# Gated linear attention feeding a gated FFN: decays of five units fetched through DRAM, a planner that counts tiling changes, and a new plan

## The chip, the cores and the metric

The kernel runs on one core of one Trainium2 chip. The metric is the device time of one execution in microseconds (us); the lower, the better.

## The reference

Two stages run one after the other. The first is a linear attention with a decay per key channel, the second a feed-forward network (FFN) whose gate is a relu. With B = 4 batches, H = 8 heads, S = 768 tokens and D = 48 channels:

```python
f = 1.0 / (1.0 + np.exp(-f_logit))
for t in range(S):
    state = f[:, :, t, :, None] * state + np.einsum('bhd,bhe->bhde', k[:, :, t], v[:, :, t])
    y[:, :, t] = np.einsum('bhd,bhde->bhe', q[:, :, t], state)
x = y.transpose(0, 2, 1, 3).reshape(B * S, H * D)      # 3072 x 384
gate = np.maximum(x @ w_gate, 0.0)                     # 384 -> 1536
val = x @ w_val
out = gate * val @ w_out                               # 1536 -> 384
```

Inputs and output are float32.

## The kernel before

**Work.** The tokens of one batch are cut into chunks of 128. Two neighbouring chunks of a batch make a unit, so there are 12 units, taken in the order `seq`: units 0 to 3 are the first pair of chunks of batches 0 to 3, units 4 to 7 the second pair, units 8 to 11 the last. Within a unit, a partition holds two neighbouring tokens, which is why most things exist twice (i = 0, 1 for the token in the partition, y = 0, 1 for the chunk).

A unit runs through these steps:
- four loads of 384 KB (f, k, q, v), queued on SP;
- exp and ln of the gate on ScalarE (L620, L622), then sums over the tokens of a chunk on TensorE ("cum", L629 and L630);
- exponentials of the sums, one for q and one for k, per i (L641, L644, L651), and the products with q and k, called hats (L663 or L669);
- the hats are turned by TensorE with an identity (L703) and copied out of PSUM as qkT, for the units in the set `pe_hats`; for the other units a DMA turns them (L725);
- scores on TensorE (L739), masked into ptm (L747 to L752);
- "total" (L759 and L763): nine small matmuls that sum the gate over a chunk; ScalarE takes the exponential of that sum as the decay `dec` (L768);
- "state" (L777, or L787 for units of `pe_hats`) sums k times v; VectorE adds the old state (`ssum`, L594) and GpSimd multiplies by the decay (`st`, L597);
- "intra" (L819, or L826 and L830) makes the attention output, which goes to xT either by a copy (the chunks in `pe_x`) or by a copy and a DMA transpose (L848).

Two units make a group of four chunks, 512 tokens. For every group the FFN runs over 12 slices j of the hidden width: three matmuls for the gate and three for val (L866), relu on ScalarE (L872), the product gT on VectorE (L878); then the output matmuls (L894), a copy into osb and a store. In group 0 the slices j = 0 to 4 are run separately for unit 0 (256 columns) and unit 1, the slices 5 to 11 for both at once.

**Order.** The instructions of every engine are in an order that `Plan.schedule` works out when the kernel is built: it plays the program forward with written-in costs (`occ`, `lat`, and `Rings` for the DMA) and always takes the operation that can start first, at a tie the one with the lower `prio`. `pace` ties the first "cum" of a unit to an FFN slice, `first` gives the order of the first loads; `wg2@f2` puts a weight behind the landing of f of unit 2. Weights are loaded and cast by DMAs that GpSimd issues. Each engine then waits on semaphores where an operand comes from elsewhere. Until a planned 24 us, matmuls on zeros ("fillers", L958) are put into planned gaps of TensorE.

TensorE works on three tilings: whole (128 rows), rows (L739 on 48 rows, L787 on 64) and columns (L819, 32 columns).

Of the kernel before, what the change touches and what calls it, by code (L numbers as in the profile page):

```python
# [13 lines left out]
class Op:  # L14
# [4 lines left out]
                 "after", "follows", "flow", "goal", "floor", "ring", "descs", "deps0", "crosses", "slack", "tiles", "port", "early", "held")  # L19

    def __init__(self, eng, emit, reads, writes, occ, lat, prio, opens=(), after=(), follows=()):
        self.eng, self.emit, self.reads, self.writes = eng, emit, reads, writes
        self.occ, self.lat, self.prio, self.opens = occ, lat, prio, list(opens)
        self.after, self.follows = list(after), list(follows)
        self.users = []
        self.inc = False
        self.sem = None
        self.val = 0
        self.start = None
        self.flow = None  # L30
        self.ring = "hw"
        self.descs = 0
        self.floor = 0.0
        self.crosses = False
        self.slack = 0.0
        self.port = False
        self.held = False
        self.early = 0
# [13 lines left out]
class Rings:  # L52
# [27 lines left out]
    def worked(self, t):  # L80
        work = t - self.now
        for p in self.PAUSES[self.passed:]:
# [5 lines left out]
    def later(self, work):  # L88
        t = self.now
        for p in self.PAUSES[self.passed:]:  # L90
# [6 lines left out]
    def next(self):  # L97
        found = None
        for r, q in self.queue.items():
            if q:  # L100
                t = self.later(self.left[r] / self.speed(r))
# [6 lines left out]
    def step(self, t, ring):  # L108
        speeds = {r: self.speed(r) for r in self.RATE}
        for r, q in self.queue.items():  # L110
            if q:
                self.left[r] -= self.worked(t) * speeds[r]
# [17 lines left out]
class Plan:  # L130
# [3 lines left out]
    EASY = 26.0  # L134
    hot_until = 0.0
# [43 lines left out]

    def schedule(self, banks):  # L180
# [9 lines left out]
        free = dict(self.free0)  # L190
        waiting = {e: [] for e in self.ENGINES}
# [34 lines left out]
        while True:  # L226
            pick = None
            for e in self.ENGINES:
                for op in waiting[e]:
# [13 lines left out]
                    key = (at, op.prio, op.idx)  # L243
# [14 lines left out]
            (at, _, _), op, slot = pick  # L258
            e = op.eng
            waiting[e].remove(op)  # L260
# [92 lines left out]
def bass_hgrn2_outer__then__ffn_reglu_kernel(  # L353
# [23 lines left out]
    wsteps = 4  # L377
    WJ = NJ // wsteps
# [25 lines left out]
    vrest = [sb(f"vrest{i}", [128, HD], BF16) for i in range(NV // 2)]  # L404
    st = [[sb(f"st{b}_{i}", [128, SW], BF16) for i in range(2)] for b in range(B)]
# [12 lines left out]
    gT = [sb(f"gT{i}", [128, NJ, GT], BF16) for i in range(NG)]  # L418
    NR = 4
# [14 lines left out]
    pl = Plan({'bc': 3, 'tp': 2, 's': 4, 'y': 1, 'kv': 2, 'f': 4})  # L434
    pl.EASY = 34
# [61 lines left out]
    for name, t, cols, value, prio in (("halves", halves, 4, 1.0, -27), ("other", other, 64, 1.0, -26), ("away", away, 16, 16.0, -26)):  # L497
# [8 lines left out]
        ["ident"], ["ident"], occ=0.25, prio=-28)  # L506
    fill("DVE", "zeros", zeros[:], 0.0, 256, -30)
# [29 lines left out]
    def load(n, u, after=()):  # L537
# [4 lines left out]
        behind = list(after) + (sent[-5:][:1] if len(sent) >= 5 else [])  # L542
        op = chain("load", "SP", lambda: sy.dma_start(dst, src), [], [f"{n}{u % NL}"], occ=0.65, lat=1.3, prio=u * 20 - 40, after=behind)
        dma(op, f"{n}{u % NL}", 1.27, 1, 1024)
# [5 lines left out]
    def load_w(nm, s, after):  # L550
        if nm == "wo":
            src = bass.AP(tensor=w_out.tensor, offset=s * WJ * 128 * DM,
                          ap=[[DM, 128], [128 * DM, WJ], [1, DM]])
            dst = wo[:, s * WJ:(s + 1) * WJ, :]
        else:
            src = bass.AP(tensor=wsrc[nm].tensor, offset=s * WJ * 128,
                          ap=[[DFF, 128], [128 * DFF, NK], [1, WJ * 128]])
            dst = (wg if nm == "wg" else wv)[:, :, s * WJ * 128:(s + 1) * WJ * 128]
        op = chain("load_w", "POOL", lambda: gp.dma_start(dst, src), [], [f"{nm}{s}"], occ=0.79, lat=2.3,
                   prio=-10 if s == 0 else 30, after=after)  # L560
        dma(op, f"{nm}{s}", 6.0 / wsteps, ring="sw")
        return op

    done = {}

    def begin(items):
        for item in items:
            item, _, behind = item.partition("@")
            need = [done[x] for x in behind.split("&")] if behind else []
# [3 lines left out]
    t4 = lambda t: t[:, 0:HD].rearrange("p (n j e) -> p n j e", n=NP, j=2)  # L573
    QROW = NQ * 4 * NP * C

# [6 lines left out]
    def new_state(kv, u, y, P):  # L582
# [4 lines left out]
        dk = [f"dec{ai}"]  # L587
# [15 lines left out]
    def unit(u):  # L603
# [11 lines left out]
        on.update({0: {'kps': True, 'qps': True, 'q0': 'POOL', 'q1': 'POOL', 'even': 'PE', 'm00': 'DVE', 'm01': 'POOL', 'm10': 'DVE', 'tk': 'DVE', 'm11': 'DVE', 'r1': 'ACT', 'tq': 'ACT', 'v11': 'DVE', 'v10': 'DVE1', 'r0': 'POOL', 'v01': 'POOL', 'v00': 'DVE', 'x1': 'ACT', 'o1': 'DVE', 'o0': 'DVE', 'x0': 'DVE'}, 1: {'kps': True, 'r0': 'ACT', 'm01': 'DVE', 'm00': 'DVE', 'tq': 'ACT', 'v11': 'DVE', 'even': 'PE', 'tk': 'DVE', 'q1': 'POOL', 'v00': 'ACT', 'm11': 'DVE', 'r1': 'DVE1', 'm10': 'POOL', 'v01': 'ACT', 'v10': 'POOL', 'q0': 'POOL', 'qps': True, 'x1': 'ACT', 'o0': 'DVE', 'o1': 'DVE', 'x0': 'DVE'}, 2: {'tk': 'ACT', 'v01': 'POOL', 'kps': True, 'r1': 'DVE1', 'r0': 'ACT', 'even': 'DVE', 'q0': 'POOL', 'v00': 'ACT', 'v10': 'ACT', 'm00': 'DVE', 'v11': 'DVE1', 'm01': 'DVE', 'm11': 'DVE', 'tq': 'ACT', 'q1': 'POOL', 'm10': 'POOL', 'qps': False, 'o1': 'DVE', 'x1': 'DVE', 'o0': 'DVE', 'x0': 'DVE'}, 4: {'v10': 'ACT', 'v01': 'ACT', 'm00': 'DVE', 'q11': 'DVE', 'q00': 'POOL', 'q01': 'POOL', 'q0': 'POOL', 'kps': True, 'even': 'DVE', 'm01': 'DVE', 'v00': 'DVE1', 'm10': 'POOL', 'q10': 'POOL', 'q1': 'POOL', 'm11': 'POOL', 'v11': 'POOL', 'qps': True, 'tq': 'DVE', 'r0': 'POOL', 'tk': 'DVE', 'r1': 'POOL', 'o1': 'DVE', 'o0': 'DVE', 'x0': 'DVE'}, 10: {'m00': 'POOL', 'm10': 'DVE', 'q0': 'DVE', 'kps': True, 'q10': 'DVE', 'm01': 'POOL', 'q11': 'DVE', 'q00': 'POOL', 'v11': 'ACT', 'even': 'DVE', 'v01': 'DVE1', 'v00': 'POOL', 'q01': 'POOL', 'q1': 'POOL', 'm11': 'DVE', 'v10': 'DVE1', 'qps': True, 'o1': 'ACT', 'o0': 'DVE'}, 9: {'v11': 'DVE1', 'v10': 'POOL', 'even': 'DVE', 'kps': True, 'q1': 'POOL', 'm10': 'DVE', 'v00': 'DVE1', 'm11': 'POOL', 'q11': 'POOL', 'm00': 'DVE', 'q00': 'POOL', 'q10': 'POOL', 'q0': 'POOL', 'q01': 'POOL', 'v01': 'ACT', 'o1': 'ACT', 'x1': 'ACT'}, 3: {'kps': True, 'm00': 'POOL', 'm11': 'POOL', 'v11': 'ACT', 'm10': 'POOL', 'tk': 'DVE', 'v01': 'POOL', 'r1': 'ACT', 'tq': 'ACT', 'q1': 'DVE', 'v00': 'DVE1', 'v10': 'ACT', 'q0': 'DVE', 'r0': 'POOL', 'm01': 'POOL', 'even': 'PE', 'qps': True, 'x0': 'DVE', 'o1': 'DVE', 'x1': 'ACT', 'o0': 'DVE'}, 5: {'q1': 'POOL', 'm00': 'POOL', 'kps': True, 'q11': 'POOL', 'v10': 'ACT', 'v00': 'ACT', 'even': 'PE', 'q01': 'POOL', 'm11': 'DVE', 'q00': 'POOL', 'q0': 'POOL', 'v11': 'DVE1', 'm01': 'DVE', 'q10': 'POOL', 'v01': 'ACT', 'm10': 'DVE', 'tq': 'DVE', 'r0': 'DVE1', 'tk': 'ACT', 'r1': 'POOL', 'qps': False, 'x0': 'ACT', 'o1': 'ACT', 'x1': 'ACT', 'o0': 'ACT'}, 11: {'q0': 'POOL', 'v01': 'ACT', 'q10': 'POOL', 'm00': 'POOL', 'q01': 'POOL', 'm11': 'POOL', 'q1': 'POOL', 'q00': 'POOL', 'kps': True, 'v11': 'POOL', 'm01': 'DVE', 'q11': 'POOL', 'even': 'DVE', 'v00': 'POOL', 'm10': 'DVE', 'v10': 'POOL', 'x1': 'ACT', 'o1': 'ACT', 'o0': 'ACT'}, 7: {'v10': 'POOL', 'kps': True, 'q1': 'POOL', 'v01': 'ACT', 'q11': 'POOL', 'm00': 'DVE', 'v11': 'DVE1', 'even': 'DVE', 'm10': 'POOL', 'm11': 'DVE', 'm01': 'DVE', 'q10': 'POOL', 'qps': False, 'q01': 'POOL', 'o1': 'DVE', 'x1': 'DVE', 'q00': 'POOL'}, 8: {'m10': 'DVE', 'v11': 'ACT', 'q01': 'POOL', 'm01': 'POOL', 'even': 'DVE', 'q0': 'POOL', 'v10': 'ACT', 'q1': 'POOL', 'm00': 'DVE', 'kps': True, 'q11': 'POOL', 'q00': 'POOL', 'qps': False, 'o0': 'DVE'}, 6: {'v10': 'DVE1', 'v01': 'DVE1', 'q10': 'DVE', 'm10': 'POOL', 'kps': True, 'q1': 'POOL', 'even': 'PE', 'q01': 'DVE', 'm00': 'POOL', 'm01': 'POOL', 'q11': 'DVE', 'q00': 'POOL', 'm11': 'DVE', 'qps': True, 'o0': 'DVE', 'o1': 'DVE'}}.get(u, {}))  # L615
# [63 lines left out]
        v4 = by_i["v"]  # L679
        for y in range(2):  # L680
            vi = vis[y]
            for i in range(2):
# [49 lines left out]
        for y in range(2):  # L732
# [9 lines left out]
            chain("scores", "PE", scores, both, sj, occ=0.26, lat=PE_L, prio=P + 5, opens=sj)  # L742
# [12 lines left out]
        tot = Bank("kv")  # L755
        ny = 1 if last else 2

        def total():
# [292 lines left out]
```

## Time and profile before

| | us |
|---|---|
| median of 3 runs (lowest, highest) | 196.26 (196.06, 196.44) |
| profiled execution, its own time | 196.28 |
| its span, first to last instruction | 194.5 |
| TensorE busy | 187.0 (96%) |
| VectorE busy | 131.1 (67%) |
| ScalarE busy | 123.2 (63%) |
| GpSimd busy | 75.2 (39%) |

The page of the profile lists, in this order: busy time by engine, the span in 40 slices, the DMA queues, the chain of work that ended last, the costliest groups of instructions, and the DMA issues. In a timeline each row has the start, the length, the engine, the source line, the operation, "out<-in" with shapes, and how many instructions were merged into the row; in brackets stands how long the engine had been idle before and what released it. SPq stands for SP's queue issuing a DMA. A row's length at TensorE includes the pipeline, so the distance between the starts of two rows is the time that the first one took from the engine.

### The profile page before, as it was taken

The numbers are of one execution on the slowest core, as the hardware profiler recorded it, in microseconds if no ns is written. First come the engines' busy times: TensorE is split into PE (matmuls) and PEld (weight loads), VectorE is DVE, ScalarE is ACT, GpSimd is POOL, SyncE is SP. The second block draws the span as 40 slices with busy tenths as digits, with TensorE's granted clock in tenths as the row PEclk, the third lists the DMA queues.
The fourth block names the chain that finished last, engine by engine and source line by source line (L and its number), as shares of the span: only waits on it lengthen the run. The fifth ranks groups of instructions, "written<-read, shape, count | busy, mean of one in ns | idle before, by whom it ended". The sixth has DMA issues, their size and how long they took to land.

```text
span 194.5 us, 4615 instructions
## 1 busy us (share of the span) xinstructions
PE 187.0 (96%) x1827; PEld 104.7 (54%) x1850; DVE 131.1 (67%) x247; ACT 123.2 (63%) x239; POOL 75.2 (39%) x105
## 2 busy tenths in 40 slices
PE   7988999999999999999999999999999999999995
PEld 2355684655655545555555555555455455544564
DVE  4589975875799896996699976337988533442310
ACT  4997769888398999959597455336364633344312
POOL 5286458058518624096468852000056210000000
PEclk9999999999999999999999999999999999999999
DMA  6999999995999899899965472201344301111113
GB/s 163 325 290 201 255 264 193 213 275 154 318 282 286 214 323 304 185 226 219 305 186 116 80 148 66 66 16 40 93 96 89 82 18 28 44 40 40 40 43 119
DMA packets 74469, 31.36 MB, mean 161 GB/s; under 512 B 66640, under 2 KB 74448, under 8 KB 74448
## 3 DMA queue, kind: packets, MB, share of 16 engines
q1 hardware_dynamic: 69648, 27.53, 55.5%
q0 software_dynamic: 4800, 3.54, 12.0%
q8 instruction: 14, 0.23, 0.5%
q14 instruction: 7, 0.06, 0.1%
HBM read 25.95 MB, written 4.72 MB: 158 GB/s over the span
## 4 chain that ended last, share of the span: by engine, by line
PE 73%; ACT 11%; DVE 10%; issue 3%; DMA 2%; POOL 0%; SPq 0%; DVEq 0%
PE ps L866 37%; PE ps L894 21%; PE ps L819 3%; PE ps L958 3%; DVE ptm L752 2%; PE ps L703 2%; ACT relu L872 2%; PE ps L739 2%; DVE hats L669 2%; DVE gT L878 2%; DMA qkT<-hats 2%; ACT ptm L747 1%; ACT expo L644 1%; ACT f_in L620 1%; ACT ps L651 1%
## 5 line engine op out<-in xcount | busy, mean ns | idle before, releaser
L878 DVE TENSOR_TENSOR gT<-relu,ps 128x512 bf16<-128x512 bf16 (+1 forms) x77 | 49.4, 649 | 33.4 <-PE ps L866 30.2
L872 ACT ACTIVATE relu<-ps 128x512 bf16<-128x512 f32 (+1 forms) x77 | 43.7, 570 | 31.5 <-PE ps L866 31.0
L866 PE MATMUL ps<-xT,wv 128*128 128x512 bf16 (+1 forms) x225 | 58.0, 365 | 0.8 <-issue 0.5
L866 PE MATMUL ps<-xT,wg 128*128 128x512 bf16 (+1 forms) x216 | 56.2, 364 | 1.1 <-DVE st L589 0.2
L894 PE MATMUL ps<-wo,gT 128*128 128x384 bf16 (+2 forms) x300 | 52.0, 320 | 0.0
L894 PEld LDWEIGHTS ps<-wo,gT 128*128 128x128 bf16 x300 | 27.8, 98 | 18.6
L866 PEld LDWEIGHTS ps<-xT,wv 128*128 128x128 bf16 x231 | 21.4, 98 | 22.3 <-DVE ptm L752 0.4
L866 PEld LDWEIGHTS ps<-xT,wg 128*128 128x128 bf16 x231 | 21.4, 98 | 19.3 <-DVE st L589 0.4
L749 POOL TENSOR_TENSOR ptm<-ptm,seen 128x512 bf16<-128x512 bf16 x20 | 22.8, 1154 | 23.1 <-ACT ptm L747 23.1
L597 POOL TENSOR_TENSOR st<-ssum,dec 128x384 bf16<-128x384 f32 x16 | 13.3, 830 | 42.7 <-DVE ssum L594 39.5
L752 DVE TENSOR_TENSOR ptm<-ps,seen 128x512 bf16<-128x512 f32 x28 | 17.8, 683 | 2.4 <-PE ps L739 2.3
L474 ACT ACTIVATE osb<-ps 128x384 f32<-128x384 f32 (+2 forms) x10 | 4.6, 459 | 16.5 <-PE ps L894 16.5
L475 DVE COPY osb<-ps 128x384 f32<-128x384 f32 x15 | 8.3, 554 | 8.3 <-PE ps L894 8.2
L669 DVE TENSOR_TENSOR hats<-k_in,ps 64x384 bf16<-64x384 f32 x24 | 13.2, 550 | 0.6 <-ACT ps L651 0.3
L747 ACT ACTIVATE ptm<-ps 128x512 bf16<-128x512 f32 x20 | 11.1, 598 | 4.1 <-PE ps L739 4.0
L669 POOL TENSOR_TENSOR hats<-q_in,expo 64x384 bf16<-64x384 f32 x12 | 11.9, 995 | 1.3 <-ACT expo L644 0.6
L651 ACT ACTIVATE ps<-ps 128x384 f32<-128x384 f32 x24 | 10.8, 484 | 0.0
L620 ACT ACTIVATE f_in<-f_in 128x768 f32<-128x768 f32 x12 | 10.1, 840 | 1.1 <-DMA f_in<-in_f_logit_dram 1.0
L474 ACT ACTIVATE xT<-ps 128x384 bf16<-128x384 f32 x11 | 6.6, 601 | 6.2 <-PE ps L819 5.9
L958 PE MATMUL ps<-zeros 128*128 128x512 bf16 x31 | 9.7, 461 | 0.6 <-DVE hats L663 0.6
L622 ACT ACTIVATE bneg<-f_in 128x768 bf16<-128x768 f32 x12 | 10.1, 841 | 0.1
L474 ACT ACTIVATE vpad<-v_in 64x384 bf16<-64x384 f32 x19 | 9.9, 520 | 0.3
(83 smaller groups left out, 200.8 us busy)
## 6 DMA issues: line engine op xcount, KB each, us to landing
f_in<-in_f_logit_dram SPq DMA_DIRECT2D x12, 384.0 KB, 5.0
v_in<-in_v_dram SPq DMA_DIRECT2D x12, 384.0 KB, 5.0
k_in<-in_k_dram SPq DMA_DIRECT2D x12, 384.0 KB, 5.0
q_in<-in_q_dram SPq DMA_DIRECT2D x12, 384.0 KB, 5.1
out_dram<-osb SPq DMA_DIRECT2D x15, 192.0 KB, 2.6
out_dram<-osb SPq DMA_DIRECT2D x16, 96.0 KB, 2.2
wg<-in_moe_w_gate_dram POOLq DMA_DIRECT2D x4, 288.0 KB, 5.7
wv<-in_moe_w_val_dram POOLq DMA_DIRECT2D x4, 288.0 KB, 6.8
```

Source lines behind the costliest of these rows:

```text
L474: return sc.activation(out, src, AF.Copy)
L597: add(e, lambda: engine[e].tensor_tensor(t4(s_new), t4(tmp), rate, ALU.mult), [key] + dk, [f"S{b}_{y}"], prio=P + 2, **(dict(occ=0.79, lat ...
L651: add("ACT", lambda i=i, ex=ex: sc.activation(bc[i].ap[:, 0:HD] if in_place else ex[:, 1, :], bc[i].ap[:, 0:HD], AF.Exp, scale=1.0), [bc[i ...
L669: op = add(e, lambda i=i, n=n, x=x, e=e, y=y, lo=lo, exps=exps: engine[e].tensor_tensor(hats[64 * i:64 * i + 64, hi, y, x, :, 0:D], by_i[n ...
L747: add("ACT", lambda pt=pt, s=sj[j]: sc.activation(pt, s.ap[:, :].rearrange("p (n t) -> p n t", n=NP), AF.Copy), [sj[j]], [f"raw{mis[y]}_{j ...
L749: add("POOL", lambda pt=pt, mask=mask: gp.tensor_tensor(pt, pt, mask, ALU.mult), [f"raw{mis[y]}_{j}", "seen"], [f"raw{mis[y]}_{j}", f"ptm{ ...
L752: add("DVE", lambda pt=pt, mask=mask, s=sj[j]: ve.tensor_tensor(pt, s.ap[:, :].rearrange("p (n t) -> p n t", n=NP), mask, ALU.mult), [sj[j ...
L866: mm = te.matmul(bank.ap[:, 0:n], wt[:, kt, j * 128:(j + 1) * 128], xT[xi][:, kt, n0:n1], start=(kt == 0), stop=(kt == NK - 1))
L872: add("ACT", lambda: sc.activation(relu[ri][:, 0:n], gate.ap[:, 0:n], AF.Relu), [gate], [f"relu{ri}"], prio=P, **act_t(n))
L878: add("DVE", lambda: ve.tensor_tensor(gT[gi][:, j, n0:n1], relu[ri][:, 0:n], val.ap[:, 0:n], ALU.mult), [val, f"relu{ri}"], [f"gT{gi}_{j}_ ...
L894: mm = te.matmul(bank.ap[:, 0:cut[1] - cut[0]], gT[gi][:, j, r * C:(r + 1) * C], wo[:, j, cut[0]:cut[1]], start=(j == 0), stop=(j == NJ - 1))
L958: return te.matmul(bank.ap[:, 0:WARM], zeros[:, 0:128], zeros[:, 0:WARM], start=True, stop=True, skip_group_check=True)
```

## The change

**Decays through DRAM.** For units 7 to 11 (the entry `td` of a unit's table) the nine matmuls of "total" and their exponential are gone. Partitions 63 and 127 of the q exponential (i = 1) hold the decay of the two chunks. SP writes these rows to a DRAM tensor `rates` and, when that has landed, reads them back as columns of 4-byte elements into `dec`, with two transfers for each chunk. Unit 7 has five such transfers; units 8 to 11 need one chunk only and have three.

**The planner.** Each TensorE operation has a mode (whole, rows or columns). At a tie in the start time the planner takes an operation of the present mode first, and a change of mode costs 0.095 us in the plan. The costs of several operations, the limits of PSUM banks by kind, the slack on a DMA's landing (1 to 1.5 us) and the pauses of the DMA queues are changed too.

**Units.** `pe_hats` loses unit 4: its hats are turned by DMAs, and its "state" is done on 128 rows. `pe_x` and `q_lined` name other units.

**Start.** The loads go in another order, up to eight in flight instead of five; the first weight is put behind k of unit 1, the ninth load, where it was behind f of unit 2, the sixth. In group 0 only the slices j = 0 to 2 are run for each unit alone.

**Plan.** `pace`, the table that says which engine does a copy, mask or product, and a few priorities are new. An added path that spreads v by matmuls (`vpe`) and one that loads weights uncast (`raw_w`) are switched on for no unit and no weight.

```diff
+    TURN = 0.095
+    STAYS = False
+    def stay(self, mode, new):
+        if mode == "whole" or new == "whole":
+            return 2
+        return 0 if new == mode else 1 if self.STAYS else 2
...
-                    key = (at, op.prio, op.idx)
+                    key = (at, self.stay(mode, op.mode) if e == "PE" else 2, op.prio, op.idx)
...
+            if e == "PE":
+                if op.mode != mode:
+                    at = max(free[e] + self.TURN, at)
+                mode = op.mode
...
-    first = 'f0 v0 f1 k0 q0 f2 wg2@f2 wg0@f2 wv0@f0 wv1@v0 k1 wg1@k1 q1 wv2@q1 v1 k2@wv0 q2 wg3@q2 wv3@v0 wo1@f0 wo0@f1 wo2@f0 wo3@f0 f3@wg2 q3@wv0 k3@wg1 v2@wo1 v3@wv0'.split()
+    first = 'f0 k0 v0 q0 v1 f1 q3 q1 k1 wg0@k1 wv0@k0 wg1@f0 wv1@k0 wg2@f0 wv2@q0 wg3@q3 wo0@k0 wv3@f0 q2 wo2@q2 wo3@k0 wo1@f1 f2 k2 f3 k3@wg0 v2 v3'.split()
-    pe_hats = {0, 1, 2, 3, 4, 5}
-    pe_x = {0, 1, 2, 3, 4, 5, 6, 7, 9, 10, 11, 12, 13, 21, 22, 23}
-    q_lined = {0, 1, 4, 7, 8, 9, 10}
+    pe_hats = {0, 1, 2, 3, 5}
+    pe_x = {0, 1, 2, 3, 4, 5, 7, 8, 9, 10, 11, 12, 13, 15, 22, 23}
+    q_lined = {0, 1, 3, 5, 7, 8, 9, 10}
...
-    pl = Plan({'bc': 3, 'tp': 2, 's': 4, 'y': 1, 'kv': 2, 'f': 4})
-    pl.EASY = 34
+    pl = Plan({'bc': 3, 'tp': 1, 's': 4, 'y': 3, 'kv': 4, 'f': 4, 'hot': 1, 'vp': 1})
+    pl.EASY = 30
...
-        behind = list(after) + (sent[-5:][:1] if len(sent) >= 5 else [])
+        behind = list(after) + (sent[-8:][:1] if len(sent) >= 8 else [])
...
+        if on.get("td") and not qb and 2 * u >= NA:
+            at = 2 * u * HD
+            op = add("SP", lambda at=at: sy.dma_start(
+                bass.AP(tensor=rates, offset=at, ap=[[HD, ny], [1, HD]]),
+                bass.AP(tensor=expo, offset=63 * EROW + (ei * 2 + 1) * 2 * HD, ap=[[64 * EROW, ny], [1, HD]])),
+                [f"expq{ei}_1"], [f"rates{u}"], occ=0.36, lat=0.9, prio=P + 2.4)
+            dma(op, f"rates{u % 4}", 0.15, 1, 2)
+            for y in range(ny):
+                for j in range(2):
+                    row = bass.AP(tensor=rates, offset=at + y * HD + j * D, ap=[[1, D], [2 * D, NP]])
+                    col = bass.AP(tensor=dec_all, offset=64 * j * DROW + (a0 + y) * NP * 2 + j, ap=[[DROW, D], [2, NP]])
+                    op = add("SP", lambda row=row, col=col: sy.dma_start(col, row, allow_slow_non_contiguous=True), [f"rates{u}"],
+                             [f"dec{a0 + y}" + "_1" * j], occ=0.5, lat=0.9, prio=P + 2.5)
+                    dma(op, f"dec{a0 + y}_{j}", 0.8, 1, 192)
+        else:
+            tot = Bank("kv")
...
-                op.slack = 1 if op.flow is not None else 0
-        for r0, r1, js in {0: [(0, 2, range(0, 5)), (2, 4, range(0, 5)), (0, 4, range(5, 12))]}.get(g, [(0, GC, range(NJ))]):
+                op.slack = 1.5 if op.flow is not None else 0
+        for r0, r1, js in {0: [(0, 2, range(0, 3)), (2, 4, range(0, 3)), (0, 4, range(3, 12))]}.get(g, [(0, GC, range(NJ))]):
...
-    pace = {4: 0, 6: 22, 9: 29, 8: 32, 10: 46, 5: 6, 7: 18, 11: 44}
+    pace = {6: 21, 10: 24, 5: 3, 8: 31, 9: 23, 11: 49}
```

More of the change, by code (lines that the diff above doesn't have):

```diff
@@ L36, in __init__ @@
         self.port = False
+        self.mode = "whole"
         self.held = False
@@ L86, in worked, with later @@
         return work
-    def later(self, work):
+    def later(self, work, ring):
         t = self.now
+        if ring == "sw":
+            return t + work
         for p in self.PAUSES[self.passed:]:
@@ L741, in scores @@
                 return mm
-            chain("scores", "PE", scores, both, sj, occ=0.26, lat=PE_L, prio=P + 5, opens=sj)
+            held = [f"{n}{(2 * u - 1) % NM}_{j}" for j in range(2) for n in ("raw", "ptm")] if on.get("pr") and u else []
+            chain("scores", "PE", scores, both + held, sj, occ=0.225, lat=PE_L, prio=P + 5, opens=sj).mode = "rows"
             for j in range(2):
```

150 lines of the change are left out of this document (104 added, 46 removed).

## The prediction

> **What bounds the kernel now.** I read the page first (its busy times and the chain that ended last), then the waits of TensorE, then the timeline of TensorE from start to end.
>
> ```profile
> span 194.5 us, 4615 instructions
> PE 187.0 (96%) x1827; PEld 104.7 (54%) x1850; DVE 131.1 (67%) x247; ACT 123.2 (63%) x239; POOL 75.2 (39%) x105
> ...
> PEclk9999999999999999999999999999999999999999
> ...
> PE 73%; ACT 11%; DVE 10%; issue 3%; DMA 2%; POOL 0%; SPq 0%; DVEq 0%
> ...
> L958 PE MATMUL ps<-zeros 128*128 128x512 bf16 x31 | 9.7, 461 | 0.6 <-DVE hats L663 0.6
> ```
>
> TensorE is the bound: busy 96% of 194.5 us, at the full granted clock in every slice, and 73% of the chain. Of the 187.0 us, 9.7 are fillers on zeros, all in the start. A busy engine can still be one that waits inside its pipeline, so the waits come next.
>
> ```profile
> PE ps L950 <- DVE zeros L462: 1.3, 1, 1.3
> PE ps L787 <- ACT qkT L474: 0.6, 1, 0.6
> ```
>
> The longest wait, 1.3 us, is the very first instruction; those with useful work behind them are 0.6 us and less (the list goes on with shorter ones). So once the FFN has begun there is next to nothing to win from waits. The time can only fall if TensorE gets less to do, loses less between its instructions, or begins earlier.
>
> ```profile
> 1.65 4.47 PE L958 MATMUL ps<-zeros 128*128 128x512 bf16 x10
> ...
> 20.38 0.50 PE L866 MATMUL ps<-xT,wg 128*128 128x256 bf16 x3 [0.22 <-DVE st L589]
> 20.98 0.50 PE L866 MATMUL ps<-xT,wv 128*128 128x256 bf16 x3
> 21.31 0.49 PE L866 MATMUL ps<-xT,wg 128*128 128x256 bf16 x3
> ...
> 184.18 7.99 PE L894 MATMUL ps<-wo,gT 128*128 128x384 bf16 x60
> ```
>
> The useful stretch reaches from 20.38, the first FFN matmul, to 184.18 + 7.99 = 192.17. After it only the last copy and store remain, 194.5 - 192.17 = 2.33 us, which the change leaves as they are. The profiled execution took 196.28 us, 1.78 more than its span and 0.02 from the median of 196.26; I keep both constant and sum against 196.28.
>
> **The change, part by part.**
>
> *Nine matmuls fewer, five times.* The cost of one "total" is the distance between starts:
>
> ```profile
> 33.41 0.17 PE L759 MATMUL ps<-away,other 128*128 128x16 bf16 x1
> 33.43 0.34 PE L763 MATMUL ps<-halves,bneg 128*128 128x4 bf16 x8
> 33.63 0.81 PE L866 MATMUL ps<-xT,wg 128*128 128x512 bf16 x3
> ```
>
> 33.63 - 33.41 = 0.22 us. Units 7 to 11 run after 20.38, where TensorE has no idle time, so the whole of it counts: 5 x 0.22 = **-1.10 us**.
>
> *Unit 4 leaves TensorE's transposes.* Its 16 transposes and its "state" in row tiling stand together:
>
> ```profile
> 55.95 1.06 PE L703 MATMUL ps<-ident,hats 128*128 128x128 bf16 x16
> ...
> 57.39 0.82 PE L866 MATMUL ps<-xT,wv 128*128 128x512 bf16 x3
> ...
> 81.09 0.50 PE L777 MATMUL ps<-vpad,hats 128*128 128x96 bf16 x8
> 81.43 0.81 PE L866 MATMUL ps<-xT,wv 128*128 128x512 bf16 x3
> ```
>
> 57.39 - 55.95 = 1.44 us go, with the two changes of tiling inside; the "state" of a unit on 128 rows, 81.43 - 81.09 = 0.34 us, comes instead: **-1.10 us**. In exchange SP issues two more DMA transposes. Those of the other units show what that can cost TensorE at worst so far:
>
> ```profile
> qkT<-hats SPq DMA_TRANSPOSE x12, 3.2
> ...
> 116.94 0.62 PE L739 MATMUL ps<-qkT 48*128 48x128 bf16 x16 [0.42 <-DMA qkT<-hats]
> ```
>
> Landing takes 3.2 us, and one of twelve was late, by 0.42 us. I put 0 to 0.42 for unit 4; the cover is FFN work of the group before, and without it the 3.2 us would be seen whole.
>
> *Changes of tiling.* Here TensorE goes from FFN to scores and back:
>
> ```profile
> 68.48 0.81 PE L866 MATMUL ps<-xT,wg 128*128 128x512 bf16 x3
> 69.23 0.62 PE L739 MATMUL ps<-qkT 48*128 48x128 bf16 x16
> 69.78 0.82 PE L866 MATMUL ps<-xT,wv 128*128 128x512 bf16 x3
> ...
> 21.73 0.41 PE L819 MATMUL ps<-ptm,vpad 128*32 128x128 bf16 x16
> 22.23 0.50 PE L866 MATMUL ps<-xT,wv 128*128 128x256 bf16 x3
> ...
> 22.99 0.35 PE L819 MATMUL ps<-qkT,st 128*32 128x128 bf16 x12
> ...
> 23.50 0.50 PE L866 MATMUL ps<-xT,wv 128*128 128x256 bf16 x3
> ...
> 157.76 0.66 PE L894 MATMUL ps<-wo,gT 128*128 128x384 bf16 x3
> ```
>
> Three wide FFN matmuls take 0.65 us in a steady run, so the scores could have begun at 69.13; they begin at 69.23. One change costs about 0.10 us. Between the start of the FFN and the end I count 54 changes in the timeline, the first at 21.73 and the last at 157.76; two of them went with unit 4 above. How many of the other 52 the new order saves cannot be read from the trace. At least the intra pairs of units 4 and 11 are now tied together (the entry `yy`), which is 4 changes, 0.4 us; if the rule joins score, state and intra work of neighbours it could be 20, 2.0 us. I take 10: **-1.0 us**. [...]
>
> *The FFN's narrow slices.* 24 matmuls on 256 columns become 12 on 512: eight runs of three at 0.33 us (20.98 to 21.31 is such a step) against four of 0.65 us. Nothing.
>
> *The start.* Weights now wait for the ninth load instead of the sixth.
>
> ```profile
> 9.07 1.11 SPq L543 DMA_DIRECT2D v_in<-in_v_dram  x1
> ...
> 10.63 1.70 POOL L559 DMA_DIRECT2D wg<-in_moe_w_gate_dram  x2 [3.86 <-DMA f_in<-in_f_logit_dram]
> ...
> v_in<-in_v_dram SPq DMA_DIRECT2D x12, 384.0 KB, 5.0
> ...
> wg<-in_moe_w_gate_dram POOLq DMA_DIRECT2D x4, 288.0 KB, 5.7
> wv<-in_moe_w_val_dram POOLq DMA_DIRECT2D x4, 288.0 KB, 6.8
> ```
>
> The ninth load was issued at 9.07 and takes 5.0 us, so the first weight is asked for at about 14.07 instead of 10.63, 3.44 us later. wg0 then lands at 14.07 + 5.7 = 19.8, wv0, issued 0.85 later, at 21.7. FFN began at 20.38, so the gates can still begin in time: four of them (the PSUM limit of the FFN) fill 4 x 0.33 = 1.3 us and val follows at 21.7. If the gates run first this costs nothing; if they alternate with val as before, up to 21.7 - 20.38 = 1.3 us. Against it: unit 0 gets k as the second load and q as the fourth, and unit 1 has its four loads by 14 us, so both intra runs of unit 1, from 21.73 to 22.23 and from 22.99 to 23.50, 1.0 us together, can move ahead of the FFN into time that fillers hold now. Bounds -1.0 to +1.3; I take **+0.2**, the middle.
>
> *The DRAM trip.* A decay now takes a write, a wait on SP, a read. Nearest row: a 96 KB store.
>
> ```profile
> out_dram<-osb SPq DMA_DIRECT2D x16, 96.0 KB, 2.2
> ...
> 100.41 0.88 ACT L644 ACTIVATE expo<-ps 128x384 f32<-128x384 f32 x2
> ...
> 106.94 0.82 POOL L597 TENSOR_TENSOR st<-ssum,dec 128x384 bf16<-128x384 f32 x1
> ...
> 142.62 0.87 ACT L644 ACTIVATE expo<-ps 128x384 f32<-128x384 f32 x2 [1.53 <-DVE ps L633]
> ...
> 150.07 0.83 POOL L597 TENSOR_TENSOR st<-ssum,dec 128x384 bf16<-128x384 f32 x1 [1.61 <-DVE ssum L594]
> ```
>
> Two trips are 4.4 us. For unit 8 the q exponentials end at 101.29 and the decay is used at 106.94: 5.6 us of cover; for unit 11 from 143.49 to 150.07, 6.6 us. So it is hidden if SP is free to issue, by a margin of about 1 to 2 us. These are 5 + 4 x 3 = 17 more DMAs on SP's queue, and the reads are behind a wait: output stores, the DMA transposes of the same units and late loads queue behind it. I take +0.3 for new stalls of this kind and of unit 4, with 0 and 2.2 (one landing seen whole) as ends.
>
> Sum: 196.28 - 1.10 - 1.10 - 1.0 + 0.2 + 0.3 = **193.6 us**.
>
> **The rivals.**
>
> *The weights are late (slower).* Place: before the first FFN matmul. If the FFN start follows the gate in full, TensorE runs fillers 3.44 us longer. The tiling gains may then also be small (0.4): 196.28 - 2.20 - 0.4 + 3.44 + 0.3 = **197.4**. It decides from a delay of about 2.6 us on, where it eats the sure savings. For it: the first weight does leave 3.4 us later. Against it: the gate weight's landing at 19.8 is still ahead of 20.38.
>
> *SP's queue (slower).* SP waits at its head for `rates` to land, 2.2 us for each of five units, with qkT transposes behind it. TensorE's order is fixed, so it stops at the scores, as it did for 0.42 us at 116.94. If the five waits are seen whole, 11 us less what covers them; if two are, 193.6 + 4.4 - 0.3 = **197.7**. [...] Against it: only a few SP instructions stand behind, and each landing has 1.5 us of slack in the plan.
>
> *VectorE takes over (no change).*
>
> ```profile
> 100.00:110.00 10.00, 9.95 (x76) 5.41 (x77) 9.72 (x18) 6.81 (x17) 8.96 (x11) 1.00 0.45 96
> ```
>
> VectorE (third pair of numbers) is busy 9.72 of 10 us while units 8 and 9 are prepared. If that stretch sets the pace, what TensorE saves for units 7 to 9 and by tilings comes back as waits. Left are unit 4's 1.10 and two totals, 0.44; with the start at its late end that is 196.28 - 1.10 - 0.44 + 1.3 = **196.0**. Against it: TensorE is busy 9.95 there.
>
> *The planner's rule does nothing.* It acts on exact ties only. Then the tiling term is 0: 194.6, inside the forecast's own range.
>
> **How the numbers follow.** The forecast with its tiling and start bounds (191.5 to 195.5) gets 0.65, late weights 0.13, SP's queue 0.09, VectorE 0.13, of which 0.06 falls below the 0.4 us, 0.05 within and 0.02 above. A difference of 0.2% (0.4 us) is about what can be told from no change here. Faster: 0.65 + 0.06 = 0.71; same 0.05; slower 0.13 + 0.09 + 0.02 = 0.24. The range goes from 191.5 to 197.4, which leaves out most of the SP case and the far ends of the others.
>
> **What would show it.** Right: no L759 and L763 for units 7 to 11, 80 transposes by L703, below 45 changes of tiling after the first FFN matmul, that matmul at 20 to 21.7 us, TensorE's waits still below 1 us each, the st of L597 released by ssum. Wrong: an FFN start at 23 us or later with more fillers than 9.7 us; the scores or st waiting for a DMA; a gap of TensorE after 100 us released by VectorE; a number of tiling changes near 52.

## The result, and the profile after

| | before | after |
|---|---|---|
| median (lowest, highest), us | 196.19 (196.06, 196.44) | 194.54 (193.87, 195.06) |
| profiled execution, its own time, us | 196.28 | 193.87 |
| span, us | 194.5 | 192.1 |
| tiling changes of TensorE, whole span / behind the first val | 62 / 53 | 51 / 39 |
| first gate, first val, end of TensorE, us | 20.38, 20.98, 192.17 | 21.65, 23.32, 189.74 |

The ratio of after to before is 0.991 (0.989 to 0.993): faster by 1.65 us, four runs each. The forecast was 193.6 within 191.5 to 197.4. All times in this document are those of fast executions; one slow execution, 200.79 us of the kernel with earlier first weights, is left out.

The page of after:

```profile
span 192.1 us, 4498 instructions
PE 183.4 (95%) x1755; PEld 101.6 (53%) x1777; DVE 129.2 (67%) x238; ACT 121.6 (63%) x233; POOL 82.5 (43%) x110
...
PEclk9999999999999999999999999999999999999999
...
GB/s 154 325 325 274 214 205 205 204 230 248 235 311 285 207 320 232 309 239 160 172 258 230 172 154 118 84 77 61 62 5 149 41 44 0 41 43 41 43 42 123
...
PE 71%; DMA 12%; DVE 8%; POOL 4%; issue 2%; ACT 1%; SPq 1%; DVEq 0%
...
L646 POOL TENSOR_TENSOR st<-ssum,dec 128x384 bf16<-128x384 f32 x16 | 13.2, 828 | 24.7 <-DMA dec<-rates 12.0
```

TensorE is still the bound, at a mean granted clock of 1.000. How much work it lost can't be read from the busy times (187.0 and 183.4): the trace of before lacks the records of 21 FFN matmuls, that of after 20. A second profile of the same kernel, the first experiment below, lacks none (it has as many matmuls as weight loads):

```profile
PE 185.5 (97%) x1777; PEld 101.8 (53%) x1777; DVE 129.2 (67%) x238; ACT 121.6 (63%) x233; POOL 82.4 (43%) x110
```

In the chain, DMA has gone from 2% to 12%. GpSimd now waits 12.0 us for the decays. Whether that matters is read from TensorE's waits (total, count, longest):

```profile
PE ps L1042 <- DVE zeros L492: 1.3, 1, 1.3
PE ps L770 <- DVE hats L712: 1.0, 2, 0.6
PE ps L952 <- DMA wv<-in_moe_w_val_dram: 0.7, 1, 0.7
PE ps L678 <- ACT bneg L671: 0.5, 1, 0.5
```

All of these stand ahead of 23.4 us. The decays are not among them. The start, in TensorE's timeline, then the end:

```profile
21.31 0.41 PE L904 MATMUL ps<-ptm,vpad 128*32 128x128 bf16 x16 [0.24 <-DVE ptm L820]
21.65 0.50 PE L952 MATMUL ps<-xT,wg 128*128 128x256 bf16 x3
22.08 0.35 PE L904 MATMUL ps<-qkT,st 128*32 128x128 bf16 x12
22.26 0.40 PE L904 MATMUL ps<-ptm,vpad 128*32 128x128 bf16 x16
23.32 0.49 PE L952 MATMUL ps<-xT,wv 128*128 128x256 bf16 x3 [0.66 <-DMA wv<-in_moe_w_val_dram]
...
181.75 7.99 PE L980 MATMUL ps<-wo,gT 128*128 128x384 bf16 x60
```

Where the time went. From the first val at 23.32 to the end at 189.74 TensorE takes 166.42 us. The kernel before reached the val at 23.50 of its own timeline and had from there 192.17 - 23.50 = 168.67 us to the end. By then it had done four narrow FFN steps that after, at its first val, still has to do (four times 0.33, 1.31 us by the rows), while after has already done two "cum" matmuls (0.33 us) that before still has to do. On equal work the stretch of before is 168.67 + 1.31 - 0.33 = 169.65 us, against 166.42: **3.2 us saved**. The start lost 1.31 - 0.33 - (23.50 - 23.32) = **0.8 us**. Together 2.4 us, the difference of the two profiled executions (196.28 - 193.87 = 2.41). The medians differ by less, because executions of after spread more widely than those of before; the last group of experiments is about that.

### The profile page after: what moved, and what is told of

It is laid out like the page before. It is cut to its first block, busy times and chain, and to the rows that moved or that the text cites. A ratio compares the mean times of both kernels' runs of the same rounds, so it can differ in the third digit from the quotient of the medians.

```text
span 192.1 us, 4498 instructions
## 1 busy us (share of the span) xinstructions
PE 183.4 (95%) x1755; PEld 101.6 (53%) x1777; DVE 129.2 (67%) x238; ACT 121.6 (63%) x233; POOL 82.5 (43%) x110
## 4 chain that ended last, share of the span: by engine, by line
PE 71%; DMA 12%; DVE 8%; POOL 4%; issue 2%; ACT 1%; SPq 1%; DVEq 0%
PE ps L952 37%; PE ps L980 23%; DMA wo<-in_moe_w_out_dram 10%; PE ps L806 3%; DMA v_in<-in_v_dram 2%; DVE hats L718 2%; PE ps L904 2%; DVE gT L964 1%; DVE hats L712 1%; DVE ptm L820 1%; POOL wo L606 1%; PE ps L770 1%; PE ps L860 1%; POOL hats L712 1%; PE ps L915 1%
## 5 line engine op out<-in xcount | busy, mean ns | idle before, releaser
L952 PE MATMUL ps<-xT,wv 128*128 128x512 bf16 (+1 forms) x223 | 58.8, 370 | 0.9 <-DMA wv<-in_moe_w_val_dram 0.7
L952 PE MATMUL ps<-xT,wg 128*128 128x512 bf16 (+1 forms) x207 | 55.4, 370 | 1.4 <-issue 0.5
L817 POOL TENSOR_TENSOR ptm<-ptm,seen 128x512 bf16<-128x512 bf16 x21 | 23.9, 1154 | 20.8 <-ACT ptm L815 20.7
L504 ACT ACTIVATE osb<-ps 128x384 f32<-128x384 f32 x13 | 6.3, 488 | 20.2 <-PE ps L980 20.2
L718 POOL TENSOR_TENSOR hats<-q_in,expo 64x384 bf16<-64x384 f32 x16 | 15.9, 994 | 5.6 <-ACT expo L693 4.6
L718 DVE TENSOR_TENSOR hats<-k_in,ps 64x384 bf16<-64x384 f32 x28 | 15.4, 552 | 1.1 <-ACT ps L700 0.6
L712 POOL TENSOR_TENSOR hats<-q_in,expo 128x384 bf16<-128x384 f32 x11 | 10.9, 1005 | 11.5 <-ACT expo L693 11.5
L815 ACT ACTIVATE ptm<-ps 128x512 bf16<-128x512 f32 x21 | 11.5, 599 | 2.5 <-PE ps L806 2.5
L505 DVE COPY osb<-ps 128x384 f32<-128x384 f32 (+2 forms) x12 | 6.3, 523 | 9.9 <-PE ps L980 9.8
L502 DVE TENSOR_REDUCE vpad<-v_in 64x384 bf16<-64x384 f32 x17 | 9.3, 545 | 4.3 <-DMA v_in<-in_v_dram 3.6
L693 ACT ACTIVATE expo<-ps 128x384 f32<-128x384 f32 x20 | 9.1, 492 | 4.6 <-DVE ps L682 3.9
L700 ACT ACTIVATE ps<-ps 128x384 f32<-128x384 f32 x22 | 10.3, 491 | 0.0
```

The costliest lines, as they stand in the source:

```text
L700: add("ACT", lambda i=i, ex=ex: sc.activation(bc[i].ap[:, 0:HD] if in_place else ex[:, 1, :], bc[i].ap[:, 0:HD], AF.Exp, scale=1.0), [bc[i ...
L712: add(e, lambda i=i, n=n, x=x, e=e, exps=exps: engine[e].tensor_tensor(hats[:, hi, i, x, :, 0:D], by_i[n][:, i, :, :], exps(), ALU.mult), ...
L718: op = add(e, lambda i=i, n=n, x=x, e=e, y=y, lo=lo, exps=exps: engine[e].tensor_tensor(hats[64 * i:64 * i + 64, hi, y, x, :, 0:D], by_i[n ...
L815: add("ACT", lambda pt=pt, s=sj[j]: sc.activation(pt, s.ap[:, :].rearrange("p (n t) -> p n t", n=NP), AF.Copy), [sj[j]], [f"raw{mis[y]}_{j ...
L817: add("POOL", lambda pt=pt, mask=mask: gp.tensor_tensor(pt, pt, mask, ALU.mult), [f"raw{mis[y]}_{j}", "seen"], [f"raw{mis[y]}_{j}", f"ptm{ ...
L952: mm = te.matmul(bank.ap[:, 0:n], wt[:, kt, j * 128:(j + 1) * 128], xT[xi][:, kt, n0:n1], start=(kt == 0), stop=(kt == NK - 1))
```

## The experiments

Each kernel was run with the kernel before on the same chip; the three sets have 196.36, 196.28 and 196.20 us as median of before. "Replanned" means that the planner made a new order after the edit, "frozen" that the order of after was kept but for the move named.

My theory after the result: TensorE's own work (the "totals", unit 4, the tiling changes) makes the gain, and late weights at the start take part of it back. Rivals: the gain is only a better-timed plan; the decays' way through DRAM or SP's queue takes something back.

### Undoing one part

**The kernel after again** (no edit).

> The changed kernel unaltered, as the yardstick for the others of this group and to see its spread. Theory 'TensorE's own work, less a late start': 194.5 us, with the first val matmul of the FFN at about 23.3 us and each us by which the weights land later showing one for one at the end of TensorE. Rival 'plan': the spread comes from somewhere after 50 us and the start is the same in a slower run.

194.33 us (193.65 to 195.25, 6 runs), ratio 0.990 (0.987 to 0.993). The gain is there again.

**Totals and exponentials back for units 7 to 11** (replanned):

```diff
-        if on.get("td") and not qb and 2 * u >= NA:
+        if False and on.get("td") and not qb and 2 * u >= NA:
```

> The decays of units 7 to 11 come from the nine matmuls and their exponential again; the rest of the changed kernel's source stays, and the planner orders it anew. Theory 'TensorE's own work': 5 x 0.22 = 1.1 us slower than the changed kernel, plus 0.1 for one more change of tiling in its order, so about 195.7. Rival 'SP's queue': the 17 transfers and their waits cost TensorE time, so the kernel is as fast or faster without them. Rival 'plan': anything within 1.5 us either way, with the five runs of nine matmuls not visible as an equal lengthening between the first FFN matmul and the end.

195.39 us (195.06 to 196.67, 12 runs), ratio 0.996 (0.994 to 0.998). That is 1.06 us above after, against 5 x 0.22 = 1.10 us. The intervals of the two ratios do not overlap, but they leave the difference open by some 0.7 us to either side, and the order is a new one; the traces below show how much of the agreement is luck.

**Unit 4 back on TensorE's transposes** (replanned):

```diff
-    pe_hats = {0, 1, 2, 3, 5}
+    pe_hats = {0, 1, 2, 3, 4, 5}
```

> Unit 4 goes back into the set whose hats TensorE turns; the planner orders anew. Theory 'TensorE's own work': 1.1 us for the transposes and the row-tiled state, which include its own two changes of tiling; the new order has nine changes more than the changed kernel behind the first FFN matmuls, so seven beyond these, 0.7 us: 1.8 us slower, about 196.3. Rival 'DMA transposes of unit 4 cost as much': no slower than the changed kernel but for the 0.7. Rival 'plan': no relation.

196.50 us (195.91 to 197.34, 12 runs), ratio 1.001 (0.999 to 1.002): 2.17 us above after, the whole gain. I had 1.8. In the trace there are 48 changes of tiling behind the first val instead of 39. Two of the nine are in the 1.10 us of the transposes; seven more are 0.7 us; a wait of 0.6 us for the hats at a "state" comes on top. Between these two plans, taking unit 4 off TensorE is worth twice its instructions; the other half is the changes of tiling and the wait that the planner's other order brings.

**No price for a change of tiling in the plan** (replanned):

```diff
-    TURN = 0.095
+    TURN = 0.0
```

> A change of tiling costs nothing in the plan and is not avoided at a tie; all else as in the changed kernel, ordered anew. The order has 42 changes behind the first FFN matmuls instead of 39. Theory 'changes cost 0.10 us each, but the planner's rule saves few of them': 0.3 us slower, about 194.8. Rival 'the rule is what saved the eight changes': 0.8 us slower or more, 195.3. Rival 'the plan is better timed with the cost in it': slower by more than the changes explain, with waits of TensorE of over 1 us in all that the changed kernel does not have.

195.50 us (195.35 to 196.93, 12 runs), ratio 0.996 (0.994 to 0.998): 1.17 us above after, where I expected 0.3. There are only three more changes (42). The larger part is waits of TensorE behind the first val, where after has none longer than 0.16 us. The three longest:

```profile
48.47 0.21 PE L871 MATMUL ps<-vpad,hats 64*128 64x96 bf16 x1 [0.21 <-DVE vrest L502]
76.53 0.82 PE L952 MATMUL ps<-xT,wg 128*128 128x512 bf16 x3 [0.22 <-ACT xT L504]
110.40 0.34 PE L860 MATMUL ps<-vpad,hats 128*128 128x96 bf16 x4 [0.46 <-DVE hats L718]
```

(It also waits 0.58 us at the first val; after waits 0.66 us there, so that is no difference.) The rule for ties does nothing by itself: with it taken out, the planner writes the same order, instruction by instruction, on every engine, with the price in the plan and without it.

**Work and waits apart.** The traces of these four kernels have all their matmuls, so TensorE's time from the first val to the end can be split. In order: after again, totals back, unit 4 back, no price; each row has the stretch, its length, TensorE's busy time and number of matmuls, the granted clock, the DMA share and GB/s:

```profile
23.18:189.52 166.34, 166.27 (x1517) 1.00 0.69 154
22.90:191.47 168.57, 167.77 (x1562) 1.00 0.69 152
23.41:192.32 168.91, 168.06 (x1541) 1.00 0.66 149
23.47:191.49 168.02, 166.96 (x1517) 1.00 0.69 152
```

Unit 4 costs 1.79 us of TensorE's own time, as 1.10 and seven changes at 0.10 would have it, and 0.78 us of idle time. The totals (45 more matmuls, one more change) cost 1.50 us of TensorE's time, 0.3 more than 1.10 and one change explain; there are also 0.73 us more of idle time, most of it one late DMA transpose of the hats, and the first val is 0.28 us earlier. So that TensorE's work costs time is shown; that the medians give 1.06 against 1.10 is luck in part. Without the price the same 1517 matmuls take 0.69 us more, of which three changes are 0.3, and TensorE idles 0.99 us more. So here the rival, a better-timed plan, is right for the larger part: in this order the price pays less by avoided changes than by planned times that hold on the chip.

### What a change of tiling costs

The order is frozen; pairs of scores or intra steps in the dense part are pulled apart (`put(b, c)` takes b out and sets it behind c):

```diff
...
+        for a, b, c in list(zip(line, line[1:], line[2:])):
+            if a.mode == b.mode != "whole" and c.mode == "whole" and a.start > 24:
+                put(b, c)
```

> The order of the kernel after, frozen, except that TensorE's pairs of neighbouring scores and intra steps behind the first FFN matmuls are pulled apart by the FFN step that stood behind them: 11 times, so 22 more changes of tiling and not one instruction more. My theory, a change costs 0.10 us: +2.2 us against the kernel after (194.3), 196.5. [...] Rival, that changes are free and that the saving of the plan was one of timing: 194.3, or a little more where a split step now comes late, which would show as a wait.

196.96 us (196.66 to 197.22, 5 runs), ratio 1.004 (1.002 to 1.005): 2.6 us above after. The trace has 59 changes behind the first val, 20 more and not 22 (two separated halves met), and one new wait of 0.6 us, for a state that VectorE makes. (2.6 - 0.6) / 20 = 0.10 us for a change; from the first val to the end, trace against trace, it is (169.58 - 166.34 - 0.64) / 20 = 0.13. One split, in TensorE's timeline:

```profile
38.70 0.40 PE L806 MATMUL ps<-qkT 48*128 48x128 bf16 x8
39.03 0.82 PE L952 MATMUL ps<-xT,wv 128*128 128x512 bf16 x3
39.78 0.40 PE L806 MATMUL ps<-qkT 48*128 48x128 bf16 x8
40.11 0.82 PE L952 MATMUL ps<-xT,wg 128*128 128x512 bf16 x3
```

From 38.70 to 40.11 are 1.41 us. The unsplit scores take 0.55 us (69.23 to 69.78 in the rows of before) and the FFN step 0.65, together 1.20: two changes more cost 0.21 us. The price in the prediction stands at 0.10 to 0.13 us.

### The start: earlier weights

**The first two weights earlier** (frozen; they go ahead of GpSimd's casts of v of unit 1 and wait for f of unit 1, the sixth load, instead of k of unit 1, the ninth):

```diff
...
+    done["wg0"].deps.pop(done["k1"])
+    done["wg0"].deps[f1] = "raw"
+    move(["wg0", "wv0"], lambda o: o.start > f1.start and o.writes[0].startswith("v_"))
```

> The changed kernel's order on every engine is kept, but for two instructions: the first two weight transfers (wg0, wv0) leave GpSimd ahead of its casts of v of unit 1 and wait for f of unit 1 (sixth load) instead of k of unit 1 (ninth). Theory 'the start is late because the weights land late': they leave about 3.5 us earlier, wv0 lands before 21 us, TensorE's 0.7 us wait before the first val matmul goes, and with the order fixed just this is gained: about 0.7 us, 193.8, less what the later loads lose. Rival 'the loads are what counts': the weights take the DMA engines from q and k of unit 1, whose scores come later, and the kernel is as slow or slower, 194.5 to 196.

196.82 us (196.57 to 199.47, 11 runs), ratio 1.005 (1.002 to 1.007): 2.5 us slower than after. My theory of the start fell. The weights come earlier, but the load of f of unit 2, asked for at 11.6 us as in after, lands later: ScalarE takes it up at 20.69 instead of 17.81. TensorE's sums for unit 2 stand ahead of the FFN and wait. A row of ScalarE, TensorE's timeline, then a table of stretches (each with PE, PEld, DVE, ACT, POOL busy, the granted clock, the DMA share and GB/s):

```profile
20.69 0.84 ACT L669 ACTIVATE f_in<-f_in 128x768 f32<-128x768 f32 x1 [2.71 <-DMA f_in<-in_f_logit_dram]
...
18.73 0.82 PE L1067 MATMUL ps<-zeros 128*128 128x512 bf16 x3
22.46 0.34 PE L678 MATMUL ps<-bneg,upto 128*128 128x384 bf16 x1 [2.91 <-ACT bneg L671]
...
24.18 0.82 PE L952 MATMUL ps<-xT,wg 128*128 128x256 bf16 x3
```
```profile
18.00:20.00 2.00, 1.37 (x19) 0.66 (x19) 1.93 (x5) 0.00 (x0) 0.80 (x2) 1.00 1.17 308
20.00:22.00 2.00, 0.00 (x0) 0.00 (x0) 1.09 (x2) 1.28 (x2) 0.21 (x1) 1.00 1.29 220
22.00:24.00 2.00, 1.54 (x29) 1.15 (x29) 0.49 (x1) 1.75 (x4) 1.03 (x1) 0.74 1.26 204
24.00:26.00 2.00, 2.00 (x45) 1.09 (x34) 1.17 (x3) 1.16 (x4) 2.00 (x4) 0.50 1.24 210
26.00:28.00 2.00, 2.00 (x18) 1.74 (x17) 1.06 (x3) 1.86 (x5) 2.00 (x4) 0.91 1.21 293
```

The hole of 2.91 us is not the only loss: behind it the granted clock is 0.74, 0.50 and 0.91 in the three windows from 22 to 28, where after has 1.00 in each, and the first gate with its change of tiling takes 0.75 us (24.18 to 24.93), where it takes 0.43 in after (21.65 to 22.08). From the first val on, this kernel takes 166.62 us, as after does.

**The first weight behind f of unit 1, replanned** (one word of `first`):

```diff
-wg0@k1
+wg0@f1
```

> Only the text of the first loads is changed: all weights start behind f of unit 1 instead of k of unit 1, and the planner orders everything anew. Theory 'the start is late because the weights land late': the FFN begins by 21 us and the kernel gains up to 1 us, 193.5. Rival 'the loads are what counts': units 1 to 3 get their data later, TensorE waits for them or runs more fillers, 195 to 198.

198.39 us (197.52 to 199.23, 6 runs), ratio 1.012 (1.009 to 1.015). The FFN begins 3.5 us earlier (first val at 19.84) and the kernel ends 4 us later. TensorE waits at other places instead:

```profile
PE ps L860 <- DVE hats L718: 2.1, 2, 1.7
PE ps L952 <- DMA wv<-in_moe_w_val_dram: 1.3, 1, 1.3
```

This order has 46 changes of tiling behind the first val, and much of it is new, so the run does not say what the earlier weight alone costs; why the hats are late in it was not followed.

**The order of wo** (frozen; the second piece of wo is asked for ahead of the third and fourth):

```diff
...
+    move(["wo1"], lambda o: o.writes[0] == "wo2")
```

> The changed kernel's order, but for one transfer: the second slice of w_out (wo1), which the output matmuls need second, leaves ahead of the third and fourth instead of behind them. In the profile of the changed kernel it lands at 44.87 us and the matmuls that need it start at 44.91. Theory 'the changed kernel's spread of 1.2 us comes from this landing': the median falls by about 0.5 us to 194.0 and the runs lie within 0.5 us. Rival 'it was in time': no difference, 194.5, same spread.

194.40 us (193.59 to 195.82, 6 runs), ratio 0.992 (0.989 to 0.995). No difference: the 10% of the chain that go to wo's landing are not a bound.

### The way through DRAM

The order is frozen; `st` of units 7 to 11 multiplies by a constant tile and waits for no decay. The transfers through DRAM are still issued, and SP still waits for them:

```diff
-        rate = dec_all[:, ai].unsqueeze(3).to_broadcast([128, NP, 2, D])
+        rate = (flat[:, :, :] if 7 <= u else dec_all[:, ai]).unsqueeze(3).to_broadcast([128, NP, 2, D])
...
+            for d in [d for d in op.deps if isinstance(d.writes[0], str) and d.writes[0].startswith("dec") and d.eng == "SP"]:
+                op.deps.pop(d)
```

> The changed kernel's order, but for the wait: for units 7 to 11 the state is multiplied by 0.5 from a tile set at the start, so that GpSimd does not wait for the decays; the output is another for that. The transfers through DRAM are still issued and waited for on SP. Theory 'the DRAM trip is hidden': GpSimd's 12 us of waiting for decays vanish and the time stays, 194.5 within 0.3. Rival 'the decays are late': faster by 0.5 us or more.

194.15 us (193.78 to 195.75, 6 runs), ratio 0.991 (0.988 to 0.993). No difference, so GpSimd's wait for the decays is hidden, although the trip is not short. Unit 11 in after, first SP's queue, then GpSimd, then TensorE:

```profile
140.02 0.25 SPq L827 DMA_DIRECT2D rates<-expo  x1
142.77 1.25 SPq L792 DMA_TRANSPOSE qkT<-hats  x1
144.06 0.59 SPq L1003 DMA_DIRECT2D out_dram<-osb  x1
144.69 1.99 SPq L792 DMA_TRANSPOSE qkT<-hats  x1
146.73 1.07 SPq L836 DMA_DIRECT2D dec<-rates  x2
...
149.30 0.83 POOL L646 TENSOR_TENSOR st<-ssum,dec 128x384 bf16<-128x384 f32 x1 [7.66 <-DMA dec<-rates]
...
154.92 0.35 PE L904 MATMUL ps<-qkT,st 128*32 128x128 bf16 x12
```

The read is issued 6.7 us after the write, because two transposes and a store stand between them in the queue, and GpSimd idles 7.66 us. But `st` is ready at 150.13 and TensorE asks for it at 154.92: 4.8 us to spare.

This run does not test the other cost, transfers and waits in SP's queue that hold up the DMA transposes behind them. The traces do: in after no wait of TensorE is put down to a transpose, and the kernel with the totals back, which has none of these transfers, has one of 0.56 us at 93.81. Scores wait for a transpose for 0.30 to 0.89 us in the profiles of nearly 196 us below; whether the transfers have a part in that is not shown.

### The spread of after

Runs of after lie between 193.6 and 195.3. One of 195.82 us was caught in the profile of the wo kernel. ScalarE there, and TensorE five us later:

```profile
78.16 0.51 ACT L700 ACTIVATE ps<-ps 128x384 f32<-128x384 f32 x1
78.74 0.49 ACT L693 ACTIVATE expo<-ps 128x384 f32<-128x384 f32 x1
80.86 0.52 ACT L504 ACTIVATE vpad<-v_in 64x384 bf16<-64x384 f32 x1 [1.64 <-DMA v_in<-in_v_dram]
81.29 0.47 ACT L700 ACTIVATE ps<-ps 128x384 f32<-128x384 f32 x1
```
```profile
85.56 0.51 PE L860 MATMUL ps<-vpad,hats 128*128 128x96 bf16 x8 [1.05 <-DVE hats L718]
...
94.34 0.62 PE L806 MATMUL ps<-qkT 48*128 48x128 bf16 x16 [0.30 <-DMA qkT<-hats]
```

ScalarE copies v of unit 8, whose load lands late; the second k exponential of unit 7 (L700 at 81.29) queues behind, so the hats of unit 7 are late, and so is TensorE's "state". In the profile of after the same copy starts at 78.74 without a wait. The profile of the constant-decay kernel (195.75 us) has the same waits (1.60 at ScalarE, 1.05 and 0.56 at TensorE). Three frozen orders test whether this is the cause. In one SP issues the load of v of unit 8 two places earlier, in one ScalarE makes the two copies behind the next two relus, in one both:

```diff
+        put(v8, f8)
...
+        for x in ("v_5_1", "v_5_0"):
+            put(next(o for o in line if o.prio == 165 and o.writes[0] == x), ref)
```

The load alone:

> The order of the kernel after, frozen, except that SP issues the load of v of unit 8 two places earlier, ahead of that unit's k and q (about 3 to 4 us earlier). My theory: the executions of the kernel after differ (193.7 to 195.3) because in some of them this load lands late; ScalarE's copies of v of unit 8 wait for it, the k exponentials of unit 7 stand behind them on ScalarE, and TensorE waits 1.1 us at the state of unit 7 and 0.3 to 0.6 us at the next scores. Then all executions come near the fast ones: median 193.8, all below 194.5, no wait of TensorE at the state of unit 7. Rival, the spread comes from the weights at the start: median 194.3 and the same spread.

194.16 us (193.50 to 194.97, 6 runs), ratio 0.990 (0.988 to 0.992).

The copies alone:

> The order of the kernel after, frozen, except that ScalarE makes its two copies of v of unit 8 behind the second of the next two relus instead of ahead of the k exponential of unit 7; the load is where it was. If the spread comes from what queues behind these copies, it goes: median 193.8, all below 194.5. If it comes from the load's use of the DMA engines or from the start, it stays: 194.3 and the same spread.

193.93 us (193.76 to 196.25, 6 runs), ratio 0.991 (0.987 to 0.994).

Both:

> Both together: the load of v of unit 8 earlier and ScalarE's copies of it later, all else as in the kernel after. If each of them takes the same wait away, the two together bring no more than one: 193.8. If each takes a part of it, this is the lower of the three. Rival as for the other two: 194.3 and the same spread.

194.07 us (193.76 to 196.26, 6 runs), ratio 0.991 (0.988 to 0.995).

The medians are 0.2 to 0.4 us lower, which the intervals do not tell from after, and the spread stays: the last two have runs at 196.25 and 196.26. The second of these was profiled, and shows another load late at another place:

```profile
82.16 0.84 ACT L669 ACTIVATE f_in<-f_in 128x768 f32<-128x768 f32 x1 [2.10 <-DMA f_in<-in_f_logit_dram]
```
```profile
24.37 0.49 PE L952 MATMUL ps<-xT,wv 128*128 128x256 bf16 x3 [1.01 <-DMA wv<-in_moe_w_val_dram]
```

ScalarE now waits for f of unit 9, and the first val is 1.05 us later than in after (24.37 against 23.32). So my theory named one place where the spread shows, not its cause. What is shown is that loads and weights land late by some 1 to 2 us in some executions, and that with this order they reach TensorE; what makes them late stays open. None of these kernels beats after by more than can be measured.

## Why the prediction was right, step by step

- **The sum**: 194.54 lies inside the range, but the range also holds the 196.19 of before, so the time alone tests little. By its own terms the range of the forecast runs from 191.4 to 195.3, not from 191.5 to 195.5. The median lies 0.9 us above the forecast: 0.6 by the start, 0.2 by fewer changes saved and 0.4 by larger stalls, less 0.2 us of saving that no term explains. The terms, one by one:
- **TensorE bounds, so its own work counts**: right. On equal work 3.2 us went, against 1.10 + 1.10 + 0.8 = 3.0 by the terms as measured, and 2.4 us came out at the end.
- **Totals, -1.10**: 1.06 in the medians; in the traces 1.50 of TensorE's time with one change inside, so the term is right to a few tenths.
- **Unit 4, -1.10**: right as the price of the instructions, too small as the price of the edit (2.17 us with what the plan makes of it). The DMA transposes of unit 4 caused no wait of TensorE in the profile of after.
- **Changes of tiling, -1.0**: the price of 0.10 us was right (0.10 to 0.13 by the split pairs). I counted 54 changes; the trace has 53, of which four lie ahead of 23.50, where the comparison begins, and two are unit 4's. So the number was 8 (47 to 39), not 10. The reason given for it was wrong: the rule for ties does nothing, as the last rival said, though the rival's 194.6 does not follow from that. The price in the plan accounts for three changes, and otherwise works by timing; with unit 4 back on TensorE there are seven more beside its own two.
- **The start, +0.2**: the term that was mis-sized, by 0.6 us. I put the landing of wg0 and wv0 at 19.8 and 21.7 from the 5.7 and 6.8 us of before. Their landing took longer:

```profile
wg<-in_moe_w_gate_dram POOLq DMA_DIRECT2D x4, 288.0 KB, 9.8
wv<-in_moe_w_val_dram POOLq DMA_DIRECT2D x4, 288.0 KB, 9.7
```

  The first of each took 6.7 and 8.0 us, so wv0, issued at 15.14, was there at about 23.2 and the val followed at 23.32. The reason is what else was under way. In before, SP issues no load between 9.07 and 19.23, and from 14 to 18 us the weights are 0.78 of the 0.80 MB moved; in after, loads go on being issued up to 13.93 and share the engines with the weights. The queues in before from 14 to 18 us, then in after from 16 to 20 (packets, MB, share; q0 is GpSimd's weights, q1 SP's loads):

```profile
q0 software_dynamic: 1062, 0.78, 128.4%
...
q1 hardware_dynamic: 1764, 0.67, 65.8%
q0 software_dynamic: 453, 0.34, 55.2%
```

  In four microseconds the weights get 0.78 MB alone and 0.34 MB beside 0.67 MB of loads. These rows show that the queues share, not how they take turns. A duration taken from one mix of transfers (5.7 us for wg) did not hold in another (9.8).
- **New stalls, +0.3**: too small in the median, and not of the kind I named. They are not at the decays; they are the late loads, from 0 in the profile of after to 0.7 us in its median (194.54 - 193.87) and 1.9 us (195.75 - 193.87) in the profile of the constant-decay kernel.
- **The DRAM trip is hidden**: right, for another reason than the 1 to 2 us of margin. For unit 11 the trip took 9.3 us (140.02 to 149.30), far more than 4.4, and for unit 7 the last two reads were issued 11.5 us after the write (79.60 and 91.09). The margin was on TensorE's side of `st`, 4.8 us for unit 11.
- **The rivals**: SP's queue did not cost what the rival feared: no wait of TensorE for a transpose in after. That the transfers cost nothing at all there is argued from the traces, not tested by a run. VectorE did not take over: behind the start no wait of TensorE for it is over 0.2 us in the profile of after. Late weights: the mechanism is there, at 0.8 us and not 3.4.
- **The signs**: 80 transposes, 41 changes behind the first gate, the first gate at 21.65, no wait of 1 us behind TensorE's first instruction: these held. One did not, and the prediction had named it as a sign of being wrong: two `st` waited for the DMA of their decays, 12.0 us together. It cost nothing, since GpSimd had time.

## What to carry to other kernels

Where the bounding engine's order is fixed and dense, its own instructions and mode changes can be priced from the distance between starts of two rows, and that price held to about 0.03 us for a change of tiling here. What cannot be priced this way is how a planner's new order meets transfers: here a landing time of 5.7 us, measured in one mix of queues, was 9.8 in another, and with two weights asked for earlier ScalarE took up f of unit 2 at 20.69 instead of 17.81 us. Before pulling a late transfer forward, look at which transfers share the DMA engines with it and which engine stands in order behind those.

## What I had not expected of the hardware

- Behind a hole of 2.91 us in TensorE the granted clock went down to 0.50, its mean over the window from 24 to 26 us. That the hole is the reason is not tested apart, but all twelve executions with this order had a mean clock of 0.983 or 0.991, where those of after had 1.0.
- GpSimd's weight loads alone moved about 200 GB/s (0.78 MB from 14 to 18 us of before), SP's loads alone 325 (2.92 MB from 5 to 14 us of after). In after a piece of wg landed in 9.8 us (median), the first ones beside SP's loads, against 5.7 in before, where SP issued no load between 9.07 and 19.23.
